# A spectral filter and SiLU MLP on one core: the first stage of two batches as one contraction over all rows, and a reordered ramp with products of zeros

## Chip, cores and metric

The kernel runs on one core of one Trainium2 chip. The metric is device time in microseconds (us). Time before the change: 2638.46 us, the median of three runs (2636.82 to 2638.56). The profile shown is of one more execution, 2635.87 us as timed, whose span in the trace is 2633.7 us.

Five engines work side by side, each through its own instruction stream in program order: TensorE (PE, its weight loads apart as PEld), VectorE (DVE), ScalarE (ACT), GpSimd (POOL) and SyncE (SP), which only issues transfers here. SP, ACT and POOL each have a queue of DMA transfers.

## The reference

The input x has 8 batches of 3008 rows and 256 channels. Each batch goes through a circular filter along its rows, and the rows of the result through a two-layer MLP with SiLU:

```
X = np.fft.rfft(x, axis=1)                       # per batch and channel, 3008 rows
Y = X * (filt_r + 1j * filt_i)[None, :, :]
y = np.fft.irfft(Y, n=3008, axis=1).reshape(24064, 256)
h = y @ w_in                                     # 256 -> 2048
out = (h / (1 + np.exp(-h))) @ w_out             # 2048 -> 256
```

x and the filter are float32. The MLP weights come as 8-byte floats and are rounded to float32 by the kernel itself.

## The kernel before

**The filter.** 3008 = 94 x 32, and the transform is done in three stages of small matrix products. Rows are written as 32*r + n, r below 94 and n below 32. *Stage 1* transforms over r for each n: it loads four n at a time (u = 0 to 7), folds row r with row r + 47 into a sum and a difference (`sums`, two DVE instructions), and multiplies both by a table `wf_t` with 47 rows: four products of 47 rows, 64 columns and 512 moving columns (`stage1`, L306), in the four quadrants of the array. Two PSUM banks of 128 x 512 are copied to SBUF (`evac`, L230 and L232; tile `t1`) and written to a scratch `d1` in DRAM by two POOL transfers (L311). *Stage 2* has six groups g: `load_t2` reads four residues per parity from `d1` (SP, L380), `forward` transforms over n (L391, tile `pb`), `multiply` (DVE, four instructions, L403) and `add` (GpSimd in batch 0, L411 and L412) apply the filter, `inverse` transforms back (L424, `pc`), `even` and `rows` (ACT L435, DVE L443) form the even and odd half, which go to a second scratch `d2` (L448). *Stage 3*, g = 0 to 7, reads `d2` (`load_t4`, L453) and transforms back over r (L465, `pd`), and `evac` puts the result into `y`. A first half of a batch needs g = 0 to 3.

Every element of `d2` feeds each `t4`, and every u of stage 1 feeds each `t2`: between the stages stands a full write and a full read of 3.1 MB.

**The MLP.** `pairs` are 48 chunks (8 batches, two halves, chunks of 256, 256 and 240 columns); each has 8 steps `jp`, one per two blocks of 128 of the 2048 hidden units. A step multiplies two 2 x 2 blocks by a scheme with seven products instead of eight, for both layers: seven products in `hidden` (L579, tiles `px` and `pyz`), three ACT copies (L587, L594, L600), SiLU (L583), combinations on DVE (L550), and seven products in `project` (L638) of the step before. It has 384 steps. The first `combine` of a chunk on DVE makes `ty` from `y` (`tokens`).

**The weights.** `load_weights(jp)` brings the raw words of two blocks j on SP (L708, L711; four transfers, 1.05 MB). `round_weights(j)` rounds a block in five DVE instructions and two ACT instructions that alternate (L721 to L729), and two GpSimd products (L734); after an odd j four GpSimd combinations make the seven blocks of `w_t` (`combine_weights`). Step jp of the first chunk needs blocks 2jp and 2jp + 1.

**Order.** Everything is ordered by hand. Before the main loop stands the *ramp*, straight code: x loads and stages 1, 2 and 3 (first half) of batch 0, with loads and roundings of weights put between. In the main loop, `put(step, rnd, piece)` places a piece at one of 8 rounds of a step; `plan` does so for each later batch, 48 steps ahead at most. Batch 1's stage 1 lies in steps 1 to 8 of batch 0; batches 2 and later use another first stage (`fold`, `stage1_fold`) for 24 of their 32 columns n and the same `sums` and `stage1` for the last two u.

**What the steps of the prediction touch.** In the ramp SP issues x in 32 transfers (L274), `d_t`, the weights of jp 0, the filters of groups 0 to 3 (16 transfers, L219), then the first `t2`. POOL issues the `d1` writes, the filters of groups 4 and 5, and then works at the products of rounding 0 and 1 and the additions. `bank` rotates six PSUM banks in the ramp; `early[0]` is None after it. In the ramp every `evac` is on ACT, later they alternate. Tiles of a tag share a fixed number of buffers (`z` has 4, `p`, `t`, `t4`, `ty`, `g`, `y` have 2, `s` has 1), and a tile waits for the last reader of its buffer.

Of the kernel before, what the change touches and what calls it, by code (L numbers as in the profile page):

```python
# [45 lines left out]
FP32 = mybir.dt.float32  # L46
# [45 lines left out]
def dft_tables():  # L92
# [10 lines left out]

    wq = np.zeros((128, 4, 32))
# [46 lines left out]
    return (wf.astype(f32), wq.astype(f32), wi.astype(f32), d.reshape(128, NS, 2, 32).astype(f32),  # L151
# [4 lines left out]
def kernel(  # L156
# [12 lines left out]
    wf_host, wq_host, wi_host, d_host, e_host = dft_tables()  # L169
    wf_dram = nc.inline_tensor(wf_host, name="wf_tbl")  # L170
    wq_dram = nc.inline_tensor(wq_host, name="wq_tbl")
# [27 lines left out]
    wf_t = cpool.tile([128, 2, 64], FP32)  # L199
    wq_t = cpool.tile([128, 4, 32], FP32)  # L200
# [5 lines left out]
    w_t = cpool.tile([128, 7, 2, NJP, 128], FP32)  # L206
    warm = cpool.tile([128, 1], FP32)
# [4 lines left out]
    def load_filters(queue, first, last):  # L212

        for j in (0, 2, 1, 3):
            s0, tau = slot_residue(0, 0, j), (1 if j % 2 == 0 else -1)
            for half in range(2):
                off, t = (s0, tau) if half == 0 else (94 - s0, -tau)
                for k, filt in enumerate((filt_r, filt_i)):
# [3 lines left out]
                                    ap=[[94 * C, 16], [t * C, last - first], [1, C]]))  # L222

    flip, early = [0], [0]

    def evac(dst, src):

        flip[0] ^= 1
        if flip[0] and early[0] is None:
            nc.vector.tensor_copy(out=dst, in_=src)  # L230
        else:
            nc.scalar.copy(out=dst, in_=src)  # L232
# [16 lines left out]
    def spectral(b):  # L249
# [5 lines left out]
        def load_x(u):  # L255


            if b == 0:
                if u == 0:
                    us["t1"] = gpool.tile([128, 2, 2, 2, C], FP32, name="t1_g", tag="g")  # L260
                if u in (0, 2):
                    xs["y"] = ypool.tile([128, 2, HALF], FP32, name=f"x_{b}_{u}", tag="y")
                if u < 4:
                    xs[u] = xs["y"][:, u % 2, 0:1024].rearrange("p (a n) -> p a n", a=2)
                elif u < 6:
                    xs[u] = t4pool.tile([128, 2, 2 * C], FP32, name=f"x_{b}_{u}", tag="t4")
                else:
                    xs[u] = x_t[u % 2]
                (nc.vector, nc.gpsimd)[u % 2].memset(xs[u][32:64], 0.0)
            else:  # L270
                xs[u] = x_t[u % 2]
            for h in range(2):
# [7 lines left out]
        def sums(u):  # L280
            if b > 0 or u % 3 == 0:
                ut = upool.tile([128, 2, 512], FP32, name=f"u_{b}_{u}", tag="u")
            else:
                if u == 1:
                    us["s"] = spool.tile([128, 2, 2, 512], FP32, name="u_s", tag="s")
                ut = us["s"][:, u % 3 - 1]
# [4 lines left out]
            if b == 1 and u + 2 < 8:  # L291
                load_x(u + 2)

        def stage1(u):
            ut = us.pop(u)
# [4 lines left out]
            else:  # L300
# [590 lines left out]
```

## Time and profile before

| what | value |
|---|---|
| time, median of 3 | 2638.46 us |
| span of the profiled execution | 2633.7 us |
| PE busy | 2559.7 us (97%) |
| DVE busy | 1716.9 us (65%) |
| ACT busy | 1101.3 us (42%) |
| POOL busy | 491.7 us (19%) |
| first product of the main loop | 112.5 us |
| first ACT copy of step 0, and of step 9 | 113.8 us, 190.6 us |
| bytes moved in the first 112 us | 25.8 MB |

The main loop takes 2521 of the 2633.7 us, the ramp the 112.5 before it. A busy share is an average over both, so the two are read apart: by slices of the span, by busy time in chosen stretches, and by the chain of waits, which follows back from the end what each instruction waited for. A matrix product of 4-byte floats shows as two records; the time from one product's start to the next one's tells more than the length of a record, since records overlap.

### The profile page before, as it was taken

The page shows a single profiled execution, that of the slowest core. Times are in us where ns is not written, and L with a number is a line of the kernel's source. Part 1 is how long each engine was busy: PE and PEld are TensorE (multiplying, and loading weights), DVE is VectorE, ACT ScalarE, POOL GpSimd, SP SyncE. Part 2 cuts the span into 40 slices and gives each one's busy share as a digit, 9 for nine tenths or more (in the row PEclk, how much of TensorE's full clock was granted, in tenths as well). Part 3 has the DMA queues.
Part 4 walks back from the last instruction along what each step waited for, and adds up shares of the span by engine and source line. Part 5 has one row for each costly group of instructions (what it writes and reads, how often), then busy time and mean ns, then how long its engine had stood idle before and what let it go on. Part 6 is the DMA issues. An engine that isn't in the chain of part 4 may idle for free.

```text
span 2633.7 us, 48160 instructions
## 1 busy us (share of the span) xinstructions
PE 2559.7 (97%) x18720; PEld 2161.6 (82%) x18720; DVE 1716.9 (65%) x3578; ACT 1101.3 (42%) x3012; POOL 491.7 (19%) x742
## 2 busy tenths in 40 slices
PE   4689999999999999999999999999999999999998
PEld 1468888888888888888888888888888888888987
DVE  4886766667666766666666666666766666555554
ACT  2344344444444444444444444444344444444443
POOL 5541112111211121112112211221112111100100
PEclk9699999999999999999999999999999999999999
DMA  9642222312223123222222222232223311211000
GB/s 263 159 118 54 72 58 70 76 55 65 70 71 74 43 65 80 66 65 61 74 60 56 73 72 63 55 82 63 65 57 73 84 45 28 55 22 21 9 16 16
DMA packets 205611, 176.11 MB, mean 67 GB/s; under 512 B 122916, under 2 KB 176932, under 8 KB 204980
## 3 DMA queue, kind: packets, MB, share of 16 engines
q1 hardware_dynamic: 184776, 120.35, 19.1%
q0 software_dynamic: 17936, 49.57, 6.1%
q8 instruction: 147, 2.41, 0.4%
q10 hardware_dynamic: 2672, 3.13, 0.4%
q14 instruction: 80, 0.66, 0.1%
HBM read 97.97 MB, written 84.41 MB: 69 GB/s over the span
## 4 chain that ended last, share of the span: by engine, by line
PE 94%; DVE 3%; DMA 1%; issue 1%; ACT 1%; SPq 0%; POOL 0%; ACTq 0%; DVEq 0%; POOLq 0%
PE acc L638 42%; PE px L579 25%; PE pyz L579 18%; PE pd L465 2%; PE pb L391 2%; PE pc L424 2%; PE pf L361 1%; PE pa L306 1%; DVE g L550 1%; DVE u L289 0%; SPq L274 0%; DMA t<-d 0%; DVE work L726 0%; DMA filt<-in_filt_r_dram 0%; DVE work L721 0%
## 5 line engine op out<-in xcount | busy, mean ns | idle before, releaser
L638 PE MATMUL acc<-g,w_t 128*128 128x256 f32 (+1 forms) x5376 | 1512.1, 375 | 0.4 <-DVE g L550 0.4
L638 PEld LDWEIGHTS acc<-g,w_t 128*128 128x128 f32 x5376 | 1021.4, 190 | 115.6 <-DVE g L550 0.8
L550 DVE TENSOR_TENSOR g<-pyz,abc 128x256 f32<-128x256 f32 (+1 forms) x1152 | 479.8, 416 | 533.9 <-ACT abc L600 294.5
L550 DVE TENSOR_TENSOR g<-g 128x256 f32<-128x256 f32 (+3 forms) x1152 | 619.6, 538 | 196.7 <-ACT g L583 183.6
L579 PE MATMUL px<-ty,w_t 128*128 128x256 f32 (+1 forms) x2304 | 688.1, 380 | 4.2 <-ACT abc L594 3.7
L583 ACT ACTIVATE g<-g 128x256 f32<-128x256 f32 (+1 forms) x1152 | 472.9, 411 | 248.4 <-DVE g L550 248.4
L550 POOL TENSOR_TENSOR s<-s 128x256 f32<-128x256 f32 (+1 forms) x329 | 259.7, 807 | 1446.3 <-DVE s L656 1435.2
L579 PEld LDWEIGHTS px<-ty,w_t 128*128 128x128 f32 x2304 | 424.2, 190 | 89.3 <-issue 30.7
L579 PE MATMUL pyz<-y,w_t 128*128 128x256 f32 (+1 forms) x1536 | 454.4, 378 | 2.2 <-DVE g L550 2.1
L579 PEld LDWEIGHTS pyz<-y,w_t 128*128 128x128 f32 x1536 | 283.5, 189 | 49.1 <-DVE g L550 7.7
L594 ACT COPY abc<-px 128x256 f32<-128x256 f32 (+1 forms) x384 | 141.3, 368 | 365.7 <-PE px L579 365.7
L583 ACT ACTIVATE g<-px 128x256 f32<-128x256 f32 (+1 forms) x384 | 145.8, 380 | 308.0 <-PE px L579 308.0
L600 ACT COPY abc<-px 128x256 f32<-128x256 f32 (+1 forms) x384 | 143.7, 374 | 311.1 <-PE px L579 310.9
L579 PE MATMUL px<-y,w_t 128*128 128x256 f32 (+1 forms) x768 | 230.0, 381 | 4.6 <-ACT g L583 2.6
L579 PE MATMUL pyz<-ty,w_t 128*128 128x256 f32 (+1 forms) x768 | 226.0, 376 | 0.1
L579 PEld LDWEIGHTS px<-y,w_t 128*128 128x128 f32 x768 | 142.1, 190 | 44.0 <-ACT g L583 15.4
L579 PEld LDWEIGHTS pyz<-ty,w_t 128*128 128x128 f32 x768 | 145.7, 190 | 17.8 <-DVE g L550 1.6
L587 ACT COPY abc<-px 128x256 f32<-128x256 f32 (+1 forms) x384 | 134.9, 351 | 2.7 <-PE px L579 1.3
L230 DVE COPY y<-pd 128x376 f32<-128x376 f32 x60 | 48.4, 807 | 97.6 <-PE pd L465 97.6
L465 PEld LDWEIGHTS pd<-wi_t,t 48*64 48x64 f32 x4096 | 69.3, 140 | 34.8 <-issue 34.1
L465 PE MATMUL pd<-wi_t,t 48*64 48x47 f32 x4096 | 77.5, 239 | 14.1 <-issue 8.1
L232 ACT COPY y<-pd 128x376 f32<-128x376 f32 x68 | 53.9, 813 | 86.8 <-PE pd L465 86.8
(68 smaller groups left out, 1354.2 us busy)
## 6 DMA issues: line engine op xcount, KB each, us to landing
t<-d SPq DMA_DIRECT2D x96, 256.0 KB
t<-d SPq DMA_DIRECT2D x128, 192.0 KB
d<-q POOLq DMA_DIRECT2D x85, 256.0 KB, 2.6
out_dram<-o SPq DMA_DIRECT2D x636, 32.0 KB
d<-tf POOLq DMA_DIRECT2D x144, 96.0 KB, 2.4
d<-t POOLq DMA_DIRECT2D x52, 192.0 KB, 3.2
xr<-in_x_dram SPq DMA_DIRECT2D x6, 1472.0 KB
x_all<-in_x_dram SPq DMA_DIRECT2D x72, 96.0 KB
```

The source lines that it names most:

```text
L230: nc.vector.tensor_copy(out=dst, in_=src)
L232: nc.scalar.copy(out=dst, in_=src)
L391: nc.tensor.matmul(out=ps[k][32 * j:32 * j + 32, ri, :], lhsT=d_t[rows, 4 * g + at, ri, :], rhs=t2[rows, at, :], start=True, stop=True)
L424: nc.tensor.matmul(out=ps[j][64 * k:64 * k + 64, a, :], lhsT=e_t[rows, g + a, k, ri, :], rhs=zs[k][rows, ri, :], start=(a == 0 and ri == 0 ...
L465: nc.tensor.matmul(out=ps[h][c0:c0 + 64, cb, i, :], lhsT=t4s[g][rows, i, 128 * cb + c0:128 * cb + c0 + 64], rhs=wi_t[rows, :], start=True, ...
L550: eng.tensor_tensor(out=out, in0=in0, in1=in1, op=op)
L579: nc.tensor.matmul(out=out, lhsT=w_t[:, c, 0, jp], rhs=rhs, start=start, stop=True, skip_group_check=True)
L583: nc.scalar.activation(out=g[:, k, 0:n], in_=g[:, k, 0:n] if src is None else src, func=AFT.Silu)
L587: nc.scalar.copy(out=sums[:, 0, 0:n], in_=xo)
L594: nc.scalar.copy(out=sums[:, 1, 0:n], in_=xo)
L600: nc.scalar.copy(out=sums[:, 2, 0:n], in_=xo)
L638: nc.tensor.matmul(out=acc[pair][i][:, h, 0:n], lhsT=w_t[:, c, 1, jp], rhs=g[:, k, 0:n], start=(jp == 0 and h == 0), stop=last, skip_group ...
```

## The change

It has six parts.

1. Stage 1 of batches 0 and 1 is one contraction over all 94 rows. A new table `wx_t` of 96 rows (two of them zeros, and rows in the order 64 to 95, 0 to 63) and 128 columns replaces fold and `wf_t`; x is loaded in 64 and 32 rows of 4 KB, two transfers for each u; there are two products of 96 rows, 128 columns and 512 moving columns for each u, no `sums` and no clearing of unused rows. Batches 2 and later keep `sums` and `wf_t` for their last two u.
2. Evictions: `evac` alternates DVE and ACT in the ramp too; in batch 1's stage 1 both copies are on ACT.
3. Loads in the ramp: the filters of groups 0 to 3 are issued by ACT, two transfers ahead of each u of stage 1; four `t2` and later four `t4` are asked for at once, two of each in the buffers of the other tag; `d_t` is loaded in two parts; filters of groups 4 and 5 come after the first `t2`; weights of jp 1 before stage 2, of jp 2 and 3 after groups 3 and 4, of jp 4 and 5 during and after stage 3.
4. Roundings: blocks 2 and 3 after groups 2 and 3, only 4 and 5 beside stage 3, and 6 to 15 in steps 0 to 5 (before: 4 to 8 ahead of stage 3 and 9 to 15 in steps 0 to 5).
5. A rounding's two work tiles are taken from the tags `z` and `p` instead of `ty`, and raw words of jp 4 and 6 from `y`.
6. `idle(n)`: n products of a zeroed block of `w_t`, 128 x 128 by 128 x 256, into the PSUM tile of `px`. There are 5 before stage 1, 16 before stage 2, 2 in each of its groups and 12 before stage 3.

The core of the diff:

```diff
 def load_x(u):
+            if b < 2:
+                for p0, r0, nr in ((32, 0, 64), (0, 64, 32)):
+                    nc.sync.dma_start(out=xs[u][p0:p0 + nr],
+                                      in_=bass.AP(tensor=x.tensor,
+                                                  offset=x.offset + (b * S + 32 * r0 + 4 * u) * C,
+                                                  ap=[[32 * C, nr], [1, 4 * C]]))
+                return
...
 def stage1(u):
+            if b < 2:
+                xt = xs.pop(u)
+                for h in range(2):
+                    nc.tensor.matmul(out=ps[h].rearrange("p n c -> p (n c)"), lhsT=wx_t,
+                                     rhs=xt[0:96, 512 * h:512 * h + 512], start=True, stop=True)
...
             for h in range(2):
-                evac(t1[:, h], ps[h])
+                if b == 1:
+                    nc.scalar.copy(out=t1[:, h], in_=ps[h])
+                else:
+                    evac(t1[:, h], ps[h])
...
-        work = typool.tile([128, 2, 512], U32, name=f"work_{j}", tag="ty")
-        e, m = work[:, 0], work[:, 1]
+        e = zpool.tile([128, 512], U32, name=f"e_{j}", tag="z")
+        m = ppool.tile([128, 512], U32, name=f"m_{j}", tag="p")
...
+    def idle(n):
+        ps = xps.tile([128, 512], FP32, name="idle", tag="x")
+        for _ in range(n):
+            nc.tensor.matmul(out=ps[:, 0:256], lhsT=zero_t[:, 0:128], rhs=zero_t, start=True, stop=True)
...
+    idle(5)
+    nc.sync.dma_start(out=d_t[:, 0:8], in_=d_dram[:, 0:8])
     weights(0)
-    load_filters(nc.sync, 0, 4)
-    for u in range(3):
-        part["sums"](u)
-    for u in range(8):
+    for u, _ in enumerate(load_filters(nc.scalar, 0, 4)):
         part["stage1"](u)
-        if u + 3 < 8:
-            part["sums"](u + 3)
-    load_filters(nc.gpsimd, 4, 2 * NG)
-    part["load_t2"](0)
-    part["load_t2"](1)
+    for g in range(2):
+        part["load_t2"](g)
+    nc.sync.dma_start(out=d_t[:, 8:NS], in_=d_dram[:, 8:NS])
     nc.sync.dma_start(out=e_t, in_=e_dram.ap())
+    for _ in load_filters(nc.gpsimd, 4, 2 * NG):
+        pass
+    for g in range(2, 4):
+        part["load_t2"](g)
     rounded(0)
     rounded(1)
+    weights(1)
+    idle(16)
     for g in range(NG):
         part["forward"](g)
...
-        if g < 3:
-            weights(1 + g)
+        if g in (3, 4):
+            weights(g - 1)
...
+        idle(2)
+        if g in (2, 3):
+            rounded(g)
     inverse_rows(part, NG - 1)
-    weights(4)
-    part["load_t4"](0)
-    part["load_t4"](1)
-    for j in range(4, 9):
-        rounded(j)
-        if j == 5:
-            weights(5)
+    idle(12)
+    for g in range(4):
+        part["load_t4"](g)
     for g in range(4):
+        if g % 2 == 0:
+            rounded(4 + g // 2)
         part["stage3"](g)
+        if g == 0:
+            weights(4)
+    weights(5)
...
-    for j in range(9, NJ):
-        put(*((j - 9, 1) if j < NJ - 1 else (5, 5)), rounded, j)
+    for j, (step, rnd) in zip(range(6, NJ), ((0, 1), (0, 5), (1, 1), (1, 5), (2, 1), (3, 1), (3, 5), (4, 1),
+                                             (4, 5), (5, 1))):
+        put(step, rnd, rounded, j)
```

## The prediction

> **What bounds the kernel now.** First the page's slices of the span (40 of 65.8 us; digits are tenths of busy time).
>
> ```profile
> PE   4689999999999999999999999999999999999998
> DVE  4886766667666766666666666666766666555554
> PEclk9699999999999999999999999999999999999999
> GB/s 263 159 118 54 72 58 70 76 55 65 70 71 74 43 65 80 66 65 61 74 60 56 73 72 63 55 82 63 65 57 73 84 45 28 55 22 21 9 16 16
> ```
>
> From the fourth slice on TensorE is full; the busy time by stretches has it at 120.00 of 120 us from 180 to 300 us and at 400 of 400 later. What the diff touches there is nothing but the tail of batch 1's first stage. So the change is worth what it does before 190 us. There I read the chain of waits in order of time (start us, us, what):
>
> ```profile
> 14.55 4.64 DMA x_all<-in_x_dram
> ...
> 27.95 6.69 DMA filt<-in_filt_r_dram
> 34.92 0.52 POOL filt L219
> 35.44 4.29 DMA filt<-in_filt_i_dram
> 39.73 7.12 DMA t<-d
> 46.99 2.04 PE pb L391 x30
> ...
> 103.62 0.88 DVE work L727
> ...
> 107.10 5.38 ACT y L232 x8
> 112.52 1.22 PE px L579 x2
> ...
> 128.00 1.73 DVE u L289 x2
> ```
>
> The ramp is four stretches: x and stage 1 (to 26 us); 21 us in which transfers alone count, with no matmul; the six groups of stage 2 (forward at 47.0, last `rows` ends at 90.1); then five roundings in a row on DVE, behind whose ScalarE halves the eight `pd` evictions queue, until the first product of the main loop at 112.5. Busy time by stretches (us of PE, PEld, DVE, ACT, POOL, then granted clock, DMA share, GB/s):
>
> ```profile
> 0.00:13.00 13.00, 6.71 (x26) 2.07 (x28) 8.82 (x13) 3.66 (x7) 7.76 (x14) 1.00 0.66 174
> 13.00:26.00 13.00, 11.24 (x40) 3.01 (x36) 5.24 (x9) 5.77 (x11) 5.33 (x11) 1.00 0.96 308
> 26.00:47.00 21.00, 1.04 (x4) 0.22 (x5) 5.00 (x10) 3.13 (x6) 14.99 (x26) 1.00 1.06 295
> 47.00:70.00 23.00, 17.54 (x223) 7.18 (x223) 14.86 (x29) 2.89 (x7) 10.18 (x15) 0.78 0.94 268
> 90.00:112.50 22.50, 8.58 (x256) 7.83 (x256) 18.98 (x26) 11.92 (x18) 16.30 (x19) 0.50 0.74 167
> ```
>
> The DMA engines are full from 13 to 70 us at about 0.3 MB/us, so the ramp is partly a matter of bytes. The clock is 0.50 at its end. In the first steps after it, DVE's chain sets the pace; the timeline has steps by their first ScalarE copy:
>
> ```profile
> 147.68 0.35 ACT L587 COPY abc<-px 128x256 f32<-128x256 f32 x1
> 156.32 0.35 ACT L587 COPY abc<-px 128x256 f32<-128x256 f32 x1
> 167.72 0.35 ACT L587 COPY abc<-px 128x256 f32<-128x256 f32 x1
> ```
>
> 8.64 us with one rounding, 11.40 with two (step 5). Later, PE-bound, a step takes 6.04 us (190.56 to 196.60), or 7.26 with a first stage.
>
> **What the Trainium skill says.** (1) "TensorE: Matmul & The Clock Gate", Part 1: the array runs at half clock until a window of about 3.4 us of activity has passed, and falls back after an idle one. The trace agrees: a `px` product (two records) starts 0.85 us after the one before it at 113.5 us and 0.43 after 121; the clock column goes 0.50 to 1.00. The column's 1.00 before 47 us is not a reading: the eight `pa` records take 2.48 us there and 1.09 at 124. (2) The same page, Part 3: products on disjoint row and column groups run at once. Agrees: eight `pa` records of 512 columns cost 1.02 us of PE, and one full product of 512 columns would cost 0.86 (twice 0.43). (3) "DMA: Bandwidth & Descriptors", "Issuing engines are not separate DMA queues": another issuing engine saves issue time, not bytes. No run here has shown the same transfers on two queues yet. (4) "SBUF — State Buffer", "SBUF: two separate sides": DVE and GpSimd exclude each other on a shared port. Agrees: the rounding's steps take 0.42 us alone, 0.95 beside GpSimd at 98 to 108 us.
>
> **The change part by part.** Sums are against this execution's span, 2633.7 us; it is 2635.9 as timed, and the timed median is 2638.5. I apply the difference to the median.
>
> *x and stage 1.* SP's x issues go from 32 (1.15 to 18.5 us, 0.45 to 0.7 each) to 16: 7 us. Eight memsets (DVE 4 x 0.91, POOL beside) and 16 sums (8 x 1.29 us on DVE) go. PE: instead of 8 x 1.99 us at half clock, 16 full products of 512 columns: 0.86 warm or 1.70 cold, so 13.8 or 27.2 us. Five zero products (4.3 us cold from about 1.3) end as x lands at about 5, so I take the warm price from about 8 us; both ends stay. Evictions, 16 x 0.57, are now half DVE's: hidden.
>
> *Filters.* The 16 issues on SP (23.4 to 38.6 us) that the first `t2` load queued behind at 38.9 go to ACT, two ahead of each eviction pair. An ACT issue of another transfer takes 0.33, SP's filter issue 0.59: 5 to 9 us on an ACT that is 44% busy there, hidden unless the ring fills. Other 16 stay on POOL and move after the `t2` loads; the products of rounding 0 and 1 (2.8 + 2.9 us at 40 to 45.8) and the `add`s queue behind them.
>
> *When can forward(0) start?* Bytes that must pass: x 3.1 MB, `d1` writes 3.1, filters 2.1, weights(0) 1.05, two `t2` 1.05, a third of `d_t` 0.26, and about 0.5 of the later filters mixed in: 11.2. At 0.308 MB/us from 2.2 us: 38.6 us. Bounds: at 0.35 (28 to 32 us reach about 0.4) 34; at 0.27, 43.7. Value 38.6, against 47.0: **-8.4**. The 16 zero products before it take 6.9 us warm (13.6 cold) from about 22: done by 29 to 36, hidden behind the loads. `rounded(0)`, `(1)`: 2 x 2.9 us of DVE in the same gap.
>
> *Stage 2.* Now 43.1 us. DVE's order gives its length: `multiply` of group 2, 3, 4, 5 starts at 63.22, 68.08, 75.82, 80.68, so 4.86 us a group (4 x 0.60, 4 x 0.43, one wait of 0.8 for ScalarE's `even`) and 2.9 more with a rounding ahead; from the last `multiply` to the last `rows` end 9.4. PE's idle 3.1 us ahead of `pb` at 64.6 and 3.0 at 77.2 end with that `multiply`, which frees the bank; they are not loads. Without other stalls, from forward(0): 2.0 to `multiply`(0), 2.45, 4 x 4.86, 2 x 2.9, 9.4 = 39.1. So what can go is 4 us: the raw words of rounding 2 (transfer of 53.4 to 57.7), now loaded earlier and rounded a group later. A warm array may shorten the tail (62 `pc` records in 5.46 us at 82.5), 1 us or so; two zero products per group, 0.9 to 1.7 us, fit in PE's idle. Bytes left for this stretch: about 9.8 MB (`t2` 2.1, `e_t` and rest of `d_t` 1.3, filters 0.5, three weights 3.15, `d2` 2.6, small tables) at 0.29: 34 us, just below. The rounding's `e` and `m` now share the tags z and p: a later `multiply` waits for a GpSimd product of 1.4 us, 0.3 to 1.5 us. Value 38; bounds 35 and 42. Last `rows` at 76.6 instead of 90.1: **-13.5** so far.
>
> *End of the ramp.* From last `rows` to first main product is now 22.4 us. All four `t4` are asked for at once: `d2` lands 2.7 us after the last `rows` (92.75 now), the first `t4` 3.3 later (96.0), the rest 1.2 MB at 0.3, 4 us; last stage 3, 1 to 2 us; eviction 0.8 (alternating engines); one rounding ahead of it on DVE instead of five: about 12.5 us, bounds 11 and 15. The 12 zero products (5 to 10 us) run while the `t4` come, and the array is warm after. **-23.4** so far: main loop at 89.1.
>
> *First steps.* Gone: 16 sums (1.75 to 2.35 us a pair at 119 to 164 us) and 8 DVE evictions of 0.6. Added: 10 roundings instead of 7 on DVE (2.35 each; on POOL 1.43 and 4.0 per pair), and PE: stage 1 costs 1.72 instead of 1.02 us, eight times: +5.6, a plain loss once PE is the bound. A step with two roundings: 8.64 - 2.0 - 0.6 + 2.5 = 8.5, still DVE's; otherwise PE's 6.04 + 1.72 + 0.1 = 7.86. Steps 0 to 8 now take 76.8 us (113.8 to 190.6). After: step 0 8.2, steps 1, 3, 4 8.5, the other five 7.9: 73.2, and 0.6 for small waits: 73.8, **-3**. Bounds: 68.9 (all PE) and 84 (four steps at 11.4). ACT gains 8 x 0.57 of evictions in an ACT at 46%: nothing. The batch 1 loads of x wait for stage 1 instead of the sums, with two steps of slack: nothing. The raw words of jp 4 to 7 are asked for behind the `t4` loads and in steps 1 and 3, each over a step (8 us, against 3 to 5 us of transfer) before its rounding: nothing. The small tables go one group later on SP, still 25 us before stage 3: nothing.
>
> Sum: 23.4 + 3 = 26.4 us less: **2612**.
>
> **Rivals.** *Bytes don't move sooner* (forward at 43.7, groups 40, end 12.5: main loop at 96): 16.3 and 1 to 3 in the steps less, **2620**. For it: DMA share 0.94 to 1.06 now. Against: GB/s only 174 in the first 13 us, 179 from 70 to 90. *Roundings in pairs* (steps 0, 1, 3, 4 at 11.4 as step 5 now): 23.4 less, 84 - 76.8 = 7.2 more, **2622**; against it, step 5 had sums and an eviction as well. *Everything is let loose* (0.35 MB/us: forward at 34, groups 35, end 12, steps near PE's floor at 70): 31.5 + 6.8 less, **2600**. *The zero products don't warm the array* (that the change doesn't do what it says), the one that ends slower: PE's order then holds 5.6 + 27.2 + 16 x 0.85 = 46.4 us before forward(0), no gain; 12 zero products in the groups add up to 10.2 (last `rows` at 99.7); the 12 after the last inverse hold stage 3 until 108, its four cold passes of 2.2 us end at 117, first main product at 117.8: +5.3, with nothing won in the steps: **2644**. It decides once the last of the 16 ends after `t2` has landed. Against: PE-busy alone warmed the array at 120 us; for: stage 1's small tiles did not, at 11.2 of 13 us.
>
> **How the numbers follow.** Likeliest 0.52 (own range 2604 to 2619); bytes 0.17 and pairs 0.05; let loose 0.20; cold 0.06, a third of it within 0.2%, which is about what a measurement of this kernel can tell from no change. Range 2598 to 2624: the bounds of DMA rate and steps, without the cold case. Faster 0.94, same 0.02, slower 0.04.
>
> **What would show it.** First `pb` at 35 to 42 us, no SP filter issue before `t2`; `pa` in pairs of full products at 0.86 apart after 8 us; last `rows` near 77; first main `px` at 85 to 93 with records at 0.43 spacing; steps 0 to 8 in 70 to 77 us, no DVE chain in steps 2, 5 to 8. A first `pb` after 44, or a ramp at clock 0.50, makes me wrong.

## The result, and the profile after

The changed kernel takes **2657.14 us** (median of 4 runs, 2654.88 to 2660.26) against 2638.51 us before (4 runs on the same chip, 2636.82 to 2639.09): ratio 1.0072, 95% interval 1.0055 to 1.009. It is slower by 19 us; the forecast was 26 us faster. The profiled execution has a span of 2658.4 us, 24.7 more than the 2633.7 of before; as timed, these two executions are 2660.26 and 2635.87, so 6 of the 24.7 us are the spread of single executions around their medians.

The slices of the span (40 of 66.5 us):

```profile
PE   6689999999999999999999999999999999999998
DVE  2575666666666676666666666666766666555554
PEclk7699999999999999999999999999999999999999
GB/s 247 160 103 64 61 74 58 56 80 65 61 66 72 61 67 70 75 72 42 66 78 62 64 71 65 56 63 74 74 57 69 79 53 28 55 22 21 9 16 16
```

From the fourth slice on it is the profile of before. The loss lies where the change is, in the first 200 us. In the busy time by stretches (us of PE, PEld, DVE, ACT, POOL, then clock, DMA share, GB/s) one row stands out:

```profile
0.00:13.00 13.00, 10.52 (x26) 5.88 (x26) 2.67 (x6) 3.24 (x5) 4.59 (x11) 1.00 0.72 194
13.00:26.00 13.00, 7.27 (x11) 2.54 (x10) 1.81 (x3) 1.39 (x3) 2.83 (x6) 0.69 0.93 290
26.00:47.00 21.00, 16.39 (x77) 9.84 (x76) 8.36 (x16) 3.92 (x7) 14.49 (x27) 0.83 0.99 257
47.00:70.00 23.00, 9.33 (x108) 4.22 (x106) 3.92 (x7) 0.37 (x1) 8.24 (x12) 0.57 1.06 252
90.00:112.50 22.50, 17.13 (x224) 11.27 (x225) 11.76 (x24) 3.79 (x8) 8.53 (x12) 0.73 0.49 128
```

Between 47 and 70 us, in the middle of stage 2, DVE worked 14.86 us before and 3.92 now, ACT 2.89 and 0.37. All four computing engines wait most of the time. The chain of waits in order of time (start us, us, what) says for what:

```profile
14.27 7.58 DMA x<-in_x_dram
...
38.16 17.88 DMA e_t<-e_tbl
...
56.06 8.02 DMA raw<-in_moe_w_out_dram
...
64.11 5.89 DMA raw<-in_moe_w_in_dram
...
70.07 0.36 ACTq L476
...
70.47 0.38 ACT q L463
```

x arrives piecemeal until 22 us; then the table `e_t`; then, of all things, a load of weights from which ScalarE's next instruction (L476, the write of a piece of `d2`) seems to be released. ScalarE's timeline shows the same gap from its side:

```profile
58.20 0.37 ACT L463 COPY q<-pc 128x256 f32<-128x256 f32 x1 [23.14 <-PE pc L452]
70.07 0.36 ACTq L476 DMA_DIRECT2D d<-q  x1
70.47 0.37 ACT L463 COPY q<-pc 128x256 f32<-128x256 f32 x1 [11.90 <-DMA raw<-in_moe_w_in_dram]
```

The data of that write were done at 59.5 us (`rows` on DVE, 58.60 + 0.88). It is given out 10.6 us later.

Marks read from the timelines of each profile, in us. "Forward" is the second group of `pb` records (46.99 before, as the forecast counts it), or the first where the products of group 0 run in one piece (r12, r13); steps run from ScalarE's first copy of one step to that of the next.

| kernel | stage 1 ends | forward | last `rows` ends | first main `px` | steps 0 to 8 | time (ratio, interval) |
|---|---|---|---|---|---|---|
| before | 25.5 | 46.99 | 90.1 | 112.52 | 76.8 | 2638.5 |
| forecast | - | 38.6 | 76.6 | 89.1 | 73.8 | 2612 |
| after | 30.5 | 42.70 | 102.3 | 121.65 | 92.2 | 2657.1 (1.0072, 1.0055 to 1.009) |
| r1 writes by GpSimd | 30.0 | 42.95 | 89.5 | 109.29 | 89.4 | 2645.3 (1.0029, 1.0018 to 1.0041) |
| r2 filters on SyncE | 20.4 | 45.82 | 98.6 | 117.67 | 88.7 | 2649.2 (1.0046, 1.0031 to 1.0061) |
| r3 no zero products | 26.5 | 40.31 | 98.0 | 117.13 | 92.1 | 2655.2 (1.0065, 1.005 to 1.008) |
| r4 roundings as before | 28.7 | 41.27 | 102.3 | 125.53 | 72.5 | 2644.4 (1.0026, 1.0016 to 1.0036) |
| r5 stage 1 a step later | 28.2 | 40.98 | 99.5 | 118.54 | 86.5 | 2653.5 (1.0062, 1.0047 to 1.0077) |
| r6 = r1 + r2 + r4 | 20.4 | 42.49 | 81.4 | 104.57 | 72.5 | 2624.0 (0.9946, 0.9932 to 0.9961) |
| r7 before + contraction | 22.6 | 43.24 | 86.5 | 108.97 | 73.9 | 2630.1 (0.9969, 0.9957 to 0.998) |
| r8 combinations on DVE | 30.0 | 42.49 | 100.7 | 119.94 | 95.5 | 2662.3 (1.0093, 1.0078 to 1.0108) |
| r9 weights' order of before | 28.7 | 41.62 | 99.3 | 118.69 | 89.5 | 2654.8 (1.0069, 1.0054 to 1.0084) |
| r13 t2 and weights of before | 28.7 | 40.30 | 96.0 | 114.93 | 89.7 | 2650.2 (1.005, 1.0034 to 1.0065) |
| r10 r6, no zero products | 21.1 | 40.78 | 80.2 | 103.37 | 72.0 | 2622.5 (0.9945, 0.9931 to 0.996) |
| r11 r6, late filters | 20.1 | 38.16 | 94.2 | 117.37 | 72.4 | 2633.8 (0.9987, 0.998 to 0.9994) |
| r12 r6, t4 first | 19.4 | 42.48 | 82.6 | 104.92 | 72.9 | 2622.5 (0.9945, 0.9928 to 0.9962) |
| r14 r12, no zero products | 22.6 | 42.74 | 83.2 | 105.61 | 72.4 | 2622.3 (0.9942, 0.9929 to 0.9954) |
| r15 r14, load order of r13 | 22.8 | 42.89 | 82.8 | 105.14 | 72.8 | 2623.7 (0.9945, 0.9932 to 0.9957) |

So of the loss (after minus before): forward -4.3, the groups of stage 2 59.6 instead of 43.1, +16.5; end of the ramp 19.3 instead of 22.4, -3.1; steps 0 to 8 +15.4. Sum +24.5 of the 24.7 us. The forward mark varies by 2 us and more between profiles with the same code ahead of it (41.0 to 43.0 in after, r1, r4, r5, r8), so a few us there say nothing; timed medians and the larger marks carry what follows.

### The profile page after: what moved, and what is told of

Same layout as the page of the kernel before. It is cut to its first block, busy times and chain, and to the rows that moved or that the text cites. A ratio compares the mean times of both kernels' runs of the same rounds, so it can differ in the third digit from the quotient of the medians.

```text
span 2658.4 us, 48101 instructions
## 1 busy us (share of the span) xinstructions
PE 2592.7 (98%) x18746; PEld 2188.6 (82%) x18746; DVE 1693.8 (64%) x3547; ACT 1098.4 (41%) x3008; POOL 483.3 (18%) x738
## 4 chain that ended last, share of the span: by engine, by line
PE 94%; DMA 3%; DVE 1%; ACT 0%; issue 0%; POOL 0%; SPq 0%; DVEq 0%; ACTq 0%; POOLq 0%
PE acc L668 42%; PE px L609 25%; PE pyz L609 18%; PE pd L496 2%; PE pc L452 2%; PE pb L419 2%; PE pf L386 1%; PE pa L319 1%; DMA e_t<-e_tbl 1%; DMA t<-d 1%; PE pa L328 0%; DMA x<-in_x_dram 0%; DMA x_all<-in_x_dram 0%; DMA raw<-in_moe_w_out_dram 0%; DMA filt<-in_filt_i_dram 0%
## 5 line engine op out<-in xcount | busy, mean ns | idle before, releaser
L609 PEld LDWEIGHTS px<-y,w_t 128*128 128x128 f32 x768 | 142.0, 190 | 46.0 <-ACT g L613 16.1
L496 PE MATMUL pd<-wi_t,t 48*64 48x47 f32 x4096 | 76.8, 238 | 7.2 <-DMA t<-d 4.2
```

The costliest lines, as they stand in the source:

```text
L496: nc.tensor.matmul(out=ps[h][c0:c0 + 64, cb, i, :], lhsT=t4s[g][rows, i, 128 * cb + c0:128 * cb + c0 + 64], rhs=wi_t[rows, :], start=True, ...
L609: nc.tensor.matmul(out=out, lhsT=w_t[:, c, 0, jp], rhs=rhs, start=start, stop=True, skip_group_check=True)
```

## The experiments

### r1: who gives out the d2 writes

The program as built explains the odd wait. Transfers given out by SyncE and by ScalarE share eight completion semaphores (lanes 0 to 7), taken in turn in one order that is fixed when the program is built; each transfer waits for the one that used its lane before. From the built programs:

```
after   SP   L743 jp 2, first half of the first raw words   waits lane 3, then uses it
        ACT  L476 first d2 write (group 0)                  waits lane 3, DVE
before  SP   L708 jp 1, third transfer                      waits lane 1, then uses it
        ACT  L448 first d2 write (group 0)                  waits lane 1, DVE
```

In that order SyncE's transfers of stage 2 stand ahead of the first write, although the code has it before several of them. In after, four transfers take lane 3 one after another: `e_t`, the fourth of jp 1, the first of jp 2, and the write. Just these stand one behind the other in the chain above, at 38.16, 56.06, 64.11 and 70.07 us, each given out when the one before it has landed. GpSimd's transfers use eight other semaphores, and the kernel gives the writes of later batches, and one of the first, to GpSimd already; 11 are left on ScalarE (the expectations say 12).

```diff
-                queue = nc.gpsimd if b > 0 or (g == NG - 1 and i == 0) else nc.scalar
+                queue = nc.gpsimd
```

> The changed kernel with one edit: in the ramp all twelve d2 writes are issued by GpSimd instead of ScalarE. Queue theory (ScalarE's write of group 0 sat from 59.4 to 70.1 us behind weight loads that SP had issued, since transfers issued by SP and ACT wait for one another in one common order, and DVE and PE stood behind it): the gap of 11.4 us ahead of the second rows goes, last rows near 92 instead of 102.3, the time near 2648. Bytes theory (the DMA engines were full from 47 to 70 us, whoever issues): the write lands no earlier, last rows at 100 to 102, time 2655 to 2658.

Measured: 2645.34 us (7 runs), 11.8 less than after; last `rows` 89.5. ScalarE's gap is gone:

```profile
57.43 0.65 ACT L463 COPY q<-pc 128x256 f32<-128x256 f32 x2 [22.92 <-PE pc L452]
62.83 0.65 ACT L463 COPY q<-pc 128x256 f32<-128x256 f32 x2 [4.75 <-PE pc L452]
```

The second pair comes 5.4 us after the first and waits for TensorE's data, not for a transfer. With the same loads, the same bytes and the same products, the last `rows` come 12.8 us earlier, against the 16.5 us that the groups had lost. **Shown**: ScalarE's writes in that order are the cause of this part. It doesn't bring the groups to the forecast: they still take 46.6 us (42.95 to 89.5), in part since another transfer holds their first inverse, `e_t`:

```profile
55.42 2.21 PE L452 MATMUL pc<-z,e_t 32*64 32x256 f32 x32 [4.78 <-DMA e_t<-e_tbl]
```

### r2: the filters back on SyncE

```diff
-    for u, _ in enumerate(load_filters(nc.scalar, 0, 4)):
-        part["stage1"](u)
+    for _ in load_filters(nc.sync, 0, 4):
+        pass
+    for u in range(8):
+        part["stage1"](u)
```

> The changed kernel with one edit: the 16 filter transfers of groups 0 to 3 are issued by SP behind the first weights, as before the change, not by ScalarE between the evictions. Queue theory (the x loads of u = 3 to 7 waited for filter transfers that ScalarE issued only after an earlier eviction): x arrives without gaps, the last stage 1 product ends at 20 to 23 us instead of 30.3, but the first t2 is then issued behind the filters at about 33 to 36, so forward starts at 40 to 44, as now (41.6): time within 4 us of 2657. Bytes theory: stage 1 still ends at 28 to 30.

Measured: 2649.16 us, 8.0 less than after; stage 1 ends at 20.4 us, ten earlier. The stretches of r2, first 26 us:

```profile
0.00:13.00 13.00, 11.78 (x26) 6.56 (x27) 2.69 (x6) 3.24 (x5) 4.61 (x11) 1.00 0.75 206
13.00:26.00 13.00, 13.00 (x45) 8.26 (x44) 4.55 (x9) 4.17 (x7) 7.81 (x16) 1.00 1.03 372
```

372 GB/s from 13 to 26 us instead of 290. The lanes again: SyncE's load of an x waits for a filter, which ScalarE gives out only after copying an earlier u, which needs an earlier x. The chain of after has such a link, ScalarE's copy, its filter, and the x given out when the filter has landed:

```profile
8.45 0.59 ACT t L247
...
9.13 4.56 DMA filt<-in_filt_i_dram
13.71 0.52 SPq L286
```

r2 puts the filters on another engine and behind all of x at once, so it doesn't part the two. The forward transform came later (45.82), as the filters stand before `t2` once more, and still the whole is faster, by more than the 4 us expected at most. Of the gain, 4.0 us stand in the ramp (`px` 117.67 instead of 121.65); the rest of the profile's difference lies in steps 0 and 5, and step 5 varies with the same code in it (10.7 us in after, 8.8 in r1 and r2).

### r3: the zero products

```diff
     def idle(n):
-        ps = xps.tile([128, 512], FP32, name="idle", tag="x")
-        for _ in range(n):
-            nc.tensor.matmul(out=ps[:, 0:256], lhsT=zero_t[:, 0:128], rhs=zero_t, start=True, stop=True)
+        return
```

> The kernel after without its 45 products of zeros; nothing else is changed, nothing that is computed is missing. Clock theory: the zero products are what lets stage 1 and the groups run at the full clock; without them the first stage ends 3 to 8 us later, the groups' products take about 2.0 instead of 1.1 us for two, and the time is 2662 to 2670. Transfer theory: TensorE waits for data in most of the ramp (it is busy 9.3 of 23 us between 47 and 70), so a slower product hides in the wait, and the 12 products before stage 3 and the 16 before the groups cost 5 to 7 us each in TensorE's own order but stand in waits as well; the time stays within 3 us of 2657. If the zero products are themselves in the way, 2648 to 2654.

Measured: 2655.2 us, 1.9 less, inside the band of the transfer theory. In r3 the clock between 47 and 70 us is 0.50 (after: 0.57), between 70 and 90 0.59 (0.76), and nothing is lost:

```profile
47.00:70.00 23.00, 9.64 (x126) 4.34 (x126) 5.79 (x11) 1.01 (x3) 4.62 (x8) 0.50 1.06 289
```

TensorE's clock isn't what this ramp waits for.

### r4 and r5: the first steps

The steps of after by ScalarE's first copy in each:

```profile
122.88 0.37 ACT L617 COPY abc<-px 128x256 f32<-128x256 f32 x1 [1.31 <-PE px L609]
137.79 0.36 ACT L617 COPY abc<-px 128x256 f32<-128x256 f32 x1
149.51 0.35 ACT L617 COPY abc<-px 128x256 f32<-128x256 f32 x1
159.36 0.35 ACT L617 COPY abc<-px 128x256 f32<-128x256 f32 x1
170.59 0.35 ACT L617 COPY abc<-px 128x256 f32<-128x256 f32 x1
182.78 0.35 ACT L617 COPY abc<-px 128x256 f32<-128x256 f32 x1
```

Steps 0, 1, 3 and 4, with two roundings each, take 14.9, 11.7, 11.2 and 12.2 us; step 2 with one takes 9.9. r4 puts the roundings where they stood before (4 to 8 ahead of stage 3, then one to a step):

```diff
-        if g % 2 == 0:
-            rounded(4 + g // 2)
         part["stage3"](g)
-        if g == 0:
-            weights(4)
...
+    for j in range(4, 9):
+        rounded(j)
...
-    for j, (step, rnd) in zip(range(6, NJ), ((0, 1), (0, 5), (1, 1), ...
-        put(step, rnd, rounded, j)
+    for j in range(9, NJ):
+        put(*((j - 9, 1) if j < NJ - 1 else (5, 5)), rounded, j)
```

> The changed kernel with the roundings placed as before the change: 4 to 8 ahead of stage 3 and 9 to 15 in steps 0 to 5, weights of jp 4 ahead of the t4 loads. Pairs theory (two roundings in a step cost 11 to 12 us a step, because the second one's DVE steps run beside GpSimd's four combinations at 0.95 instead of 0.42 us and the SiLU of the step queues behind it): steps with one rounding fall to 8 to 9 us, steps 0 to 8 take 78 to 82 instead of 92.2, the end of the ramp grows from 19.3 to 26 to 29, time 2650 to 2656. Rival (the steps are slow because batch 1's first stage lies a step earlier, waits for x, and costs more PE): steps 0 to 8 stay at 88 to 92, time 2662 to 2668.

Measured: 2644.44 us (9 runs), 12.7 less, better than the band of either theory. Steps 0 to 8 take 72.5 us, 19.7 less than in after and 4.3 less than before; stage 3 becomes longer for it (`px` 125.53 instead of 121.65). A step with one rounding and a first stage takes 7.8 us: TensorE's own 6.04 + 1.72. Over the stretch TensorE is full:

```profile
126.00:190.00 64.00, 61.88 (x232) 43.56 (x232) 42.23 (x84) 33.21 (x82) 30.66 (x44) 0.96 0.39 113
```

Steps 1 to 4 take 32.1 us instead of 44.9 (step 2, with one rounding in both, 7.8 instead of 9.9, so it had carried work of the pair before it). **Shown**: pairs of roundings cost steps 1 to 4; the larger products of stage 1 aren't what made these steps long. Step 0 is another matter: it falls from 14.9 to 8.2 us, but r4 also asks for batch 1's x earlier (116.59 instead of 121.28 us), and TensorE doesn't wait for it there. r5 looks at that wait alone.

r5 takes another piece of the diff by itself. The hunk in `plan` doesn't only drop the sums, it puts batch 1's stage 1 one step earlier, into steps 0 to 7. TensorE in after, step 0:

```profile
128.83 3.75 PE L319 MATMUL pa<-x_all,wx_t 96*128 96x512 f32 x4 [3.33 <-DMA x_all<-in_x_dram]
```

SyncE could ask for that x only at 121.28, behind the weights of jp 5.

```diff
-                put(at + u - 48, 3, part["stage1"], u)
+                put(at + u - 47, 3, part["stage1"], u)
```

> The changed kernel with batch 1's stage 1 one step later, in steps 1 to 8 as before the change. If the wait for x in step 0 (3.3 us on PE and a cold clock after it) is what the earlier place costs: step 0 falls from 14.9 to 10 to 11 us, steps 0 to 8 from 92.2 to 88 to 90 although step 8 now holds a stage 1 (+1.7), time 2653 to 2655. If pairs of roundings alone set the steps: no change, 2656 to 2659.

Measured: 2653.48 us, 3.7 less, though the intervals of the two kernels overlap. The profile is clearer: step 0 takes 9.1 instead of 14.9 us, with two roundings in it as before; step 8, which now holds a first stage, takes 7.8 instead of 6.0, steps 1 to 4 are unchanged.

### r6: do the three add up?

The edits of r1, r2 and r4 together.

> The kernel after with three changes at once: the 12 writes of the first group's d2 pieces given out by GpSimd instead of ScalarE, the four filter loads back on SyncE before the first t2, and the roundings of weights placed as in the kernel before (five before stage 3, one to a step). If the three losses are separate, the gains of the single runs add: 2657.1 - 11.8 - 8.0 - 12.7 = 2624.6, which would be 14 us under the kernel before. If they are partly the same wait seen three times (the lanes of transfers), the sum is smaller: 2630 to 2640. Marks if they add: last group ended by 86 to 90 us, the first step by 113 to 115, steps 0 to 8 in 72 to 75 us.

Measured: 2624.02 us (4 runs, 2619.99 to 2627.29), as the sum of the three gains asks (2624.6): the losses are separate. This is the change with three bad placements taken out (batch 1's stage 1 stays a step earlier), and it beats before by 0.54% (interval 0.39 to 0.68%). The stretch that stood still in after:

```profile
47.00:70.00 23.00, 18.01 (x295) 9.24 (x282) 19.92 (x40) 4.96 (x12) 17.82 (x28) 0.90 1.09 319
```

The groups take 38.9 us (42.49 to 81.4), which is the forecast's 38. r1 alone had 46.6; what is between them comes with the filters, the only other edit ahead of these groups: the first inverse starts at 48.27 and no longer waits for `e_t`. Why `e_t` lands late where ScalarE gives out the filters wasn't traced further. Only the end of the ramp is long, 23.2 us, as five roundings stand in it again.

### r7: the contraction alone, in the kernel before

```diff
-        if u + 3 < 8:
-            part["sums"](u + 3)
...
-                put(at + u - 48, 5, part["sums"], u)
                 put(at + u - 47, 3, part["stage1"], u)
```

with `wx_t`, x in 4 KB rows and the two products of after for batches 0 and 1 (`wf_t` loaded in the first group). Nothing else is moved.

> The kernel before with the first part of the change alone: stage 1 of batches 0 and 1 as one contraction over 96 rows, x in rows of 4 KB, no sums and differences for these two batches; its stage 1 stays in steps 1 to 8, filters, writes and roundings stay as they are, wf_t is loaded in the first group. Theory: the contraction itself does no harm; DVE loses 16 sums of about 1.1 us in the ramp and the steps, steps 1 to 4 fall from 8.6 to about 8.0 us, stage 1 of the ramp ends some us earlier, the first forward stays near 46 us since the filters still go ahead of t2: 2633 to 2637. Rival: the products over all rows, 64 more columns for PE at a cold clock, sit on the path of the steps: 2639 to 2645.

Measured: 2630.05 us (7 runs), 8.2 less than the 2638.2 of before beside it, more than expected. Steps 1 to 4 fall from 8.6 to 7.8 to 8.3, stage 1 of the ramp ends 3 us earlier, the last group 3.6 earlier. The rival (TensorE's larger products on the path) is out.

### r8: does GpSimd slow the second rounding of a pair?

In step 3 of after, DVE's second rounding (columns: start us, us, what; then, in brackets, the wait ahead of it) beside GpSimd's four combinations of the same pair, against the first:

```profile
162.33 0.69 DVE L761 SCALAR_TENSOR_TENSOR m<-raw,m 128x512 f32<-128x512 uint32 x1 [0.36 <-ACT m L757]
162.95 0.43 DVE L762 TENSOR_SCALAR e<-e 128x512 uint32<-128x512 f32 x1
...
166.69 1.21 DVE L761 SCALAR_TENSOR_TENSOR m<-raw_y,m 128x512 f32<-128x512 uint32 x1
167.82 0.94 DVE L762 TENSOR_SCALAR e<-e 128x512 uint32<-128x512 f32 x1
```

r8 gives those combinations to DVE:

```diff
-        combine(gp, w(S1), w(S3), w(A22), ALU.add)
+        eng = v if jp > 2 else gp
+        combine(eng, w(S1), w(S3), w(A22), ALU.add)
```

(and the other three alike).

> The kernel after with one thing changed: for the blocks of weights rounded from stage 3 on, the four long combinations that GpSimd makes are made by DVE as well, so that GpSimd doesn't work beside a rounding. Contention theory (the second rounding of a pair takes 4.7 instead of 2.9 us because GpSimd works beside it): the second rounding falls to about 3 us, plus the four combinations of 0.4 to 0.7 us each, so a pair costs as much DVE work as before or up to 2 us less: steps 1, 3 and 4 within 9.5 to 12, time 2650 to 2657. Order theory (two blocks of DVE work in one step are too much for it, whoever shares the port): steps 1, 3 and 4 get longer by the combinations' 2 to 4 us, time 2658 to 2668.

Measured: 2662.25 us, 5.1 more than after, inside the band of the order theory; of the steps that it named only step 1 grows as it said (by 2.2 us; steps 3 and 4 by 0.6 and 0.1). The rounding is fast again, and a new wait stands behind it:

```profile
145.55 0.69 DVE L761 SCALAR_TENSOR_TENSOR m<-raw_y,m 128x512 f32<-128x512 uint32 x1 [0.42 <-ACT m L757]
146.16 0.43 DVE L762 TENSOR_SCALAR e<-e 128x512 uint32<-128x512 f32 x1
...
148.84 1.56 DVE L580 TENSOR_TENSOR w_t<-w_t 128x256 f32<-128x256 f32 x4 [1.52 <-POOL w_t L769]
150.31 0.41 DVE L580 TENSOR_TENSOR g<-pyz,abc 128x256 f32<-128x256 f32 x1
```

DVE waits 1.52 us for GpSimd's product, then needs 1.56 for the combinations, and the step's `g` queues behind both: steps 0 and 1 grow to 16.0 and 13.9 us. So the contention is real (0.69 against 1.21 us), and ending it this way costs more than it brings. What the contention costs by itself stays open.

### r9 and r13: which loads hold the first write

r9 undoes the move of the weights' loads, r13 also the four `t2` asked for at once:

```diff
-    weights(1)
     idle(16)
...
-        if g in (3, 4):
-            weights(g - 1)
+        if g < 3:
+            weights(1 + g)
```

> The kernel after with one part undone: the weights of jp 1, 2 and 3 are asked for after the forward transforms of groups 0, 1 and 2, as in the kernel before, instead of before stage 2 and after groups 3 and 4. ScalarE keeps the writes of the d2 pieces. Order theory (the first d2 write waits, by the fixed order of transfers, for a load of weights that SyncE can give out only after group 2's products): with the loads ahead of that point the first write goes out by 62 us instead of 70, the last group ends at 92 to 97 instead of 102.3, and the time is 2645 to 2652. Byte theory (what holds the groups is the amount moved ahead of them): 2 MB of weights earlier make the groups wait longer, the last group ends at 102 to 108 and the time is 2656 to 2664.

r9: 2654.84 us. The write goes out at 66.88 instead of 70.07, the last group ends at 99.3, each 3 us earlier; both theories missed. In r9 ScalarE waits for another late transfer, the `t2` of group 4:

```profile
66.88 0.36 ACTq L476 DMA_DIRECT2D d<-q  x1
67.28 0.37 ACT L463 COPY q<-pc 128x256 f32<-128x256 f32 x1 [10.14 <-DMA t<-d]
```

r13 in addition:

```diff
-    for g in range(2, 4):
-        part["load_t2"](g)
...
-            if g + 2 < NG and (b > 0 or g > 1):
+            if g + 2 < NG:
```

> The kernel after with the load order within stage 2 as in the kernel before: two t2 asked for ahead of it and each next one after a forward transform, weights of jp 1, 2 and 3 after groups 0, 1 and 2. ScalarE keeps the writes of the d2 pieces, filters stay on ScalarE. By the built order of transfers, the first d2 write then stands eight behind the second half of the t2 of group 3, which can be given out right after the products of group 1. Order theory: the first write goes out by 58 to 63 us instead of 70, the last group ends at 91 to 97 instead of 102.3, the time is 2645 to 2652. Rival (the order isn't what holds the write; ScalarE and the transfers are slow in this ramp anyhow): the first write stays at 66 to 71 us and the time at 2653 to 2658.

r13: 2650.2 us, the write at 63.35:

```profile
63.35 0.36 ACTq L474 DMA_DIRECT2D d<-q  x1
63.75 0.37 ACT L461 COPY q<-pc 128x256 f32<-128x256 f32 x1 [6.19 <-DMA t<-d]
```

From the first write to the end of the last group it is 32.3 us in after, 32.4 in r9 and 32.6 in r13: each us that the write goes out earlier is a us of the groups. The order theory holds. 6.7 us of the late write come from the load order within stage 2 (70.07 to 63.35). In the built programs of all three, lane 3 goes from `e_t` to this write: over two loads in after, over the fourth of jp 1 and the `t2` of group 4 in r9, over the `t2` of group 3 alone in r13. There the write still waits 4.9 us behind its data (58.5), against 1.9 for a load of weights in the kernel before.

### r10, r11, r12, r14, r15: what is left in r6

r10 is r6 with the edit of r3.

> The kernel with the three corrections (2624.0 us) without its 45 products of zeros; nothing that is computed is missing. In the kernel after the products of zeros were worth nothing (2655.2 without, 2657.1 with), perhaps because TensorE waited for other engines in most of the ramp anyhow. If that is the reason, they may be worth something here, where the waits are shorter: stage 1 ends some us later than 20.4, groups take longer, 2627 to 2632. If the ramp is bound by transfers here too, no change: 2622 to 2626.

2622.52 us: no change. The zero products aren't worth anything here either.

r11 moves the 16 filter loads on GpSimd behind the additions of group 0.

```diff
-    for _ in load_filters(nc.gpsimd, 4, 2 * NG):
-        pass
...
             part["add"](g, k)
+        if g == 0:
+            for _ in load_filters(nc.gpsimd, 4, 2 * NG):
+                pass
```

> The kernel with the three corrections, in which GpSimd asks for the filters of groups 4 and 5 (2 MB in rows of 1 KB) only after the additions of group 0 instead of ahead of stage 2. Byte theory (the first forward transform waits for all that is moved beside the first two t2): it starts at 33 to 37 us instead of 40.8; but 16 issues of about 0.55 us on GpSimd then stand before the additions of group 1, which give back 5 to 9 us of it: time 2619 to 2626. If t2 is late for another reason (its own writes and the reads behind them), the first forward stays at 40 us and the time is 2626 to 2633.

2633.81 us (20 runs), 9.8 more than r6: both bands missed, the second narrowly. The forward transform came 4.3 us sooner (38.16), as the byte theory said, but GpSimd's issues wait for transfers too, since its eight semaphores are taken in turn as well and the ninth filter waits for the first:

```profile
51.81 0.53 POOL L233 DMA_DIRECT2D filt<-in_filt_r_dram  x1 [3.33 <-DMA filt<-in_filt_r_dram]
...
57.82 0.73 POOL L439 TENSOR_TENSOR z<-z,p 128x256 f32<-128x256 f32 x1
```

The 16 loads hold GpSimd from 44.26 to 57.8 us, 13.5 instead of the 9 of the expectation, and the additions of group 1 behind them: the last group ends 12.8 us later. In r6 they took 12.1 us too, at 22.35 to 34.4, when no additions waited.

r12 asks for the reads of `d2` ahead of the weights of jp 4.

```diff
-    weights(4)
     for g in range(4):
         part["load_t4"](g)
-    for j in range(4, 9):
+    weights(4)
+    for j in range(4, 8):
         rounded(j)
...
         part["stage3"](g)
+        if g == 1:
+            rounded(8)
```

> The kernel with the three corrections, with the four reads of d2 for stage 3 asked for ahead of the weights of jp 4 (as in the kernel after) and the rounding of block 8 after the second of the four products of stage 3. In the run before, the reads landed 7 and 14 us after the last write, beside 1 MB of weights. If the bytes beside them are the cause, stage 3 starts 3 to 4 us earlier and the end of the ramp (87.7 to 104.6, 17 us) falls to 13 or 14: 2619 to 2622. If the reads are slow by themselves, or DVE's roundings set the end of the ramp, the time stays at 2623 to 2627.

2622.46 us; from first `pd` to first `px` it takes 16.1 us against 16.8, not 13: missed. The first `pd` comes 6.3 us after the last `rows` in both, so the weights asked for ahead of the reads didn't hold it. DVE works through roundings without a gap there in r6 (84 to 100.7 us, most instructions at 0.94 to 1.2 us beside GpSimd) and evicts behind them, so by the trace those set the end of the ramp. It fits that with three roundings fewer there (after, r1) the end takes 19.3 and 19.8 us instead of 23.2.

r14 is r12 without the zero products; r15 is r14 with the load order of r13.

> The kernel with the three corrections (writes of d2 pieces by GpSimd, filters on SyncE, roundings as before), with the reads of d2 ahead of the weights of jp 4 and without the products of zeros; nothing that is computed is missing. If the two small gains (2622.5 each against 2624.0, neither sure) are real and add: 2619 to 2622. If they are noise: 2622 to 2625.

> The same kernel with the load order within stage 2 as in the kernel before (two t2 at once, weights after groups 0, 1 and 2). If the four early t2 are worth what the forecast gave them (about 5 us in the groups) once nothing waits behind them, this is slower: 2625 to 2630. If they are worth nothing: within 2 us of the run before it.

2622.25 and 2623.66 us: the small gains don't add, and the early `t2` are worth nothing that can be measured, in either direction, once no write waits behind them.

## Why the prediction was wrong

The direction was wrong. By its own steps:

- *x and stage 1*: the contraction is good (r7, 8.2 us by itself).
- *Filters*, "hidden unless the ring fills": **failed.** ScalarE's issues interlock with SyncE's x through the lanes; 8.0 us (r2). They also made `e_t` late for the groups (r1 against r6).
- *Forward(0)* at 38.6: 42.70, and 41.0 to 43.0 in like profiles, inside its bounds (34 to 43.7). The term was sized 2 to 4 us too well.
- *Stage 2*, 38 us: **failed**, 59.6, the largest error. DVE's order gives the 38 us only where neither the writes nor `e_t` wait (r6, 38.9); with the writes alone freed it is 46.6 (r1). What was missed is that moved SyncE loads stand ahead of ScalarE's writes: a wait that the sum had at nothing and that r1 measures at 12.8 us. The trace of before showed it, on ScalarE:

```profile
57.72 0.34 ACTq L448 DMA_DIRECT2D d<-q  x1
58.11 0.37 ACT L435 COPY q<-pc 128x256 f32<-128x256 f32 x1 [3.21 <-DMA raw<-in_moe_w_in_dram]
```

A copy of `pc` has no use for raw words; the write ahead of it did wait for them. The prediction saw that transfer (53.4 to 57.7) and booked it as DVE's wait for rounding 2, to be gained by moving the loads. Moving them made the wait 11.9 us. It also counted the bytes of `e_t` but not when it lands: 17.9 us after its issue in after, where it holds the first inverse by 4 us and is the first link of the chain to the write.
- *End of the ramp*, 12.5 us: 19.3. Up to the first `pd` it was right (6.2 us against 6.0). The rest took 13.1 instead of 6.5: the last piece of stage 3's products starts only at 119.12, after a gap for which the trace names no releaser.

```profile
119.12 1.61 PE L496 MATMUL pd<-wi_t,t 48*64 48x47 f32 x49 [2.85 <-issue]
```

The cause of this stays open.
- *First steps*, 73.8 us: **failed**, 92.2. "A step with two roundings 8.5" measured 11.2 to 12.2 in steps 1, 3 and 4; to step 0, which holds two as well, the sum gave 8.2, and it took 9.1 with neither its wait for x nor a first stage (r5). The sum took one rounding off and put one on as DVE instructions; it left out the second rounding's stretching beside GpSimd (4.7 instead of 2.9 us) and, by the timeline, the order in which the step's `g` and SiLU wait behind it. How much each costs isn't shown. The rival "pairs" (11.4 a step) was the right one for these steps and got 0.05. With single roundings the steps take 72.5 (r4), better than forecast, at the 7.8 us that the sum had for steps bound by TensorE.
- *"Batch 1 loads of x wait for stage 1, with two steps of slack: nothing"*: **failed**, by misreading the diff: stage 1 was moved a step earlier, and in step 0 TensorE waits 3.3 us for x; 3.7 us of the time by r5, with overlapping intervals.
- *Zero products*: whether they warm the array didn't matter (r3, r10). The one rival that forecast a slower kernel gave a cold array as the cause, and r3 rules that out: that it had the sign right is luck.

With the failed placements undone (r6) the rest of the change is worth 14 us. Of what is still missing to the forecast, 10.7 us are the end of the ramp (23.2 against 12.5): in these runs it was shorter only with roundings put into the steps, where a pair costs more than it saves (r4: 3.9 us longer in the ramp, 12.8 shorter in steps 1 to 4). On the Trainium skill's point cited in the prediction from "DMA: Bandwidth & Descriptors" ("Issuing engines are not separate DMA queues"): it names issue time as all that another engine saves; here the choice of issuing engine moved 11.8 us (r1) and, together with the place of the loads, 8.0 us (r2), through waits and not through issue time.

## What to carry to other kernels

When a load is moved on one queue, look in the built program at which transfers of other queues take a completion semaphore after it; a copy or a write that the trace shows "released by" a transfer it doesn't use is the sign. Keep writes that others wait for off a queue whose turn depends on loads that can be late, and price a step with two pieces of side work from the measured step that had two, not from the sum of their instructions. An early request is no gain by itself (r15 against r14), and a product that warms the array was worth nothing here, where the array waited.

## What the runs showed of the hardware

- Moving 11 writes of 256 KB from ScalarE to GpSimd, with all loads and bytes the same, made the kernel 11.8 us faster (r1). In these programs the transfers of SyncE and ScalarE share eight completion semaphores, those of GpSimd have eight others.
- 16 filter loads in a row on GpSimd took 0.49 to 0.56 us each for the first eight, then waited for their own earlier transfers, 13.5 us in all (r11).
- `e_t`, asked for at 38.01 us, held the first inverse until 55.42 where ScalarE gave out the filters (r1); asked for at 37.14, it no longer held the one at 48.27 where SyncE did (r6).
- 45 products of zeros on TensorE made it 1.9 and 1.5 us longer, with the waits of after and without them (r3, r10); the intervals overlap, so this can't be told from nothing.
- In step 3 of after a rounding on DVE takes 2.9 us alone and 4.7 beside GpSimd's combinations; single instructions 0.69 and 1.21 us. This agrees with what the prediction drew from the Trainium skill, "SBUF — State Buffer", "SBUF: two separate sides".
